# Block-sparse attention and a gated expert layer on one core: turning P by transposing transfers from the second batch on

## The chip, the cores and the metric

The kernel runs on one core of a Trainium2 chip. The metric is the device time of one launch in microseconds (us), the median of several runs. Engines are named as in the profile: PE is the matmul engine (PEld its weight loads), DVE and ACT are the vector and the scalar engine, POOL is GpSimd, SP only issues transfers.

## The reference

Attention over 4 batches, 8 heads, 768 positions, head width 64. Positions lie in 24 blocks of 32. A query block sees its own block and both neighbours, the first and the last block, and three sampled blocks of its own; the first and the last query block see everything. The result is laid out as 3072 tokens of 512 features and goes through a gated layer of width 1536.

```
scores = q @ k.T / sqrt(64); masked where the block pattern says so
attn   = softmax(scores);  x = attn @ v          # -> [3072, 512]
out    = (sigmoid(x @ w_gate) * (x @ w_val)) @ w_out
```

Input and output are float32; the kernel works in float16 with float32 sums.

## The kernel before

**An order that is written out by a planner.** The kernel doesn't write its instructions in the order in which they will run. It declares operations (`P(name, engine, duration, function, deps, prio, acq, rel)`), each with an engine, an assumed duration, a priority and the buffers that it takes and gives back. `Planner.run` (line 69) then plays them through with these durations: at each step it takes the engine that can start first and, of its ready operations, the one of lowest priority number. The order that comes out is fixed in the program for each engine. At run time an engine takes its instructions in just that order, and waits where an input isn't there yet. A transfer is assumed to end `dma` after its issue, plus 1.8 us.

**Attention, by batch.** `attention(b, ...)` (line 430) declares a batch. Batch b has the priority base 10 b, so batches follow each other, with the loads of the next ones ahead (`PREP`). K, Q and V come in through POOL's queue, cast to float16, into three stage buffers `stg`. PE turns K and Q tile by tile (L456), and copies put them into `KT` and `QT` (L466 to L474). `QT` holds zeros in half of its rows, so that one matmul treats two heads. V is reordered by DVE (`vsh`, L486) and written to a scratch tensor in HBM (`scr`, L495, four issues on SP), from which SP reads it back: neighbouring blocks as windows into `V1` (L542), the three sampled blocks one by one into `V2` (L587, with the block number in a register). `V1` and `V2` exist once for even and once for odd batches. `VN` is the whole V of a batch, for the dense rows (L500).

The 22 sparse query blocks of a batch go in 12 steps of one or two blocks (`S0` for batch 0, `S1` for the others; `S1` puts the blocks at the edges first). For each block PE writes the mask with four matmuls from `mrow` (L608) and adds the scores with eight (L614), in an array shape of 128 by 64. A block takes one bank of PSUM; two banks (`spool`) serve for it. DVE finds the row maxima (`mx`, L626), ACT takes the exponential (`ex`, L635), DVE the reciprocal (L643), and POOL or DVE scales P (`sl`, L651, L654). Then P must be turned, so that its columns lie on partitions: PE transposes it against an identity, four 128x128 pieces per block (`tp`, L666), and DVE or ACT copies the piece from PSUM to `PTS` (`te`, L673). PE forms P V (`pv`, L686), and ACT or DVE copies the result to `XT` (`xe`, L701).

The first and the last query block are the dense rows. They are treated for two heads at a time: scores against all of K (L714), maximum, exponential, scale (`dsc` to `dsl`), six transposes into PSUM (`dtp`, L751), a copy to `DPT` (L756), six matmuls with `VN` (`dpv`, L764). In batches 1 to 3 they have the lowest priority numbers of their batch, in batch 0 they come after two thirds of it.

**The expert layer.** The 24 tiles of 128 tokens are cut into `GROUPS`. A group's gate and value matmuls (L814, 12 column blocks of 4 matmuls each) have 128, 256 or 512 columns; tanh on ACT (L822), the product on DVE (L827), then the output matmuls (L840) and a store per tile from one of two buffers `YS` (L847 to L854). The groups have priorities above 1000, so the plan uses them to fill PE where attention leaves it idle, once their tiles are done.

Of the kernel before, what the change touches and what calls it, by code (L numbers as in the profile page):

```python
# [18 lines left out]
BLK = 32  # L19
# [29 lines left out]
class Planner:  # L49
# [19 lines left out]
    def run(self, switch=0.095, dma_lat=1.8):  # L69
# [112 lines left out]
def kernel(  # L182
# [28 lines left out]
    cst = np.zeros((1, NB, 8), np.float32)  # L211
# [3 lines left out]
    cst_h = nc.inline_tensor(cst, name="bb_cst")  # L215

# [8 lines left out]
    def sb(name, shape, dt=f16):  # L225
# [5 lines left out]
    ones = sb("ones", [128, 128], bf16)  # L231
    cst_t = sb("cst", [1, NB, 8], f32)
    sbi = sb("sbi", [1, NB * 3 * 2], i32)
    kidx = sb("kidx", [1, 128], i32)
    vidx = sb("vidx", [1, 128], i32)
# [7 lines left out]
    QT = [sb(f"QT{r}", [128, NP, NB + 1, 64]) for r in range(2)]  # L243
# [4 lines left out]
    VN = sb("VN", [128, 6, DM])  # L248
    V1 = {(r, x): sb(f"V1{r}{x}", [128, n, DM]) for r in range(2) for x, n in (("A", 4), ("B", 3))}
    V2 = {(r, x): sb(f"V2{r}{x}", [128, n, DM]) for r in range(2) for x, n in (("A", 4), ("B", 3))}  # L250
    NKG = 4
    KG = [[sb(f"KG{r}{s}", [128, NP, 160]) for s in range(NKG)] for r in range(2)]
    NPB = 6
    PB = [sb(f"P{s}", [128, 2, 256]) for s in range(NPB)]
# [3 lines left out]
    PTS = [sb(f"PTS{s}", [128, 1024]) for s in range(2)]  # L258
    DP = [sb(f"DP{s}", [128, S]) for s in range(2)]
    DPT = [sb(f"DPT{s}", [128, S]) for s in range(2)]  # L260
# [9 lines left out]
        [(0, 0), (0, 5), (1, 0), (1, 5)],  # L270
        [(1, 1), (1, 2), (1, 3), (1, 4)],
        [(2, 0), (2, 5), (2, 1), (2, 2)],
        [(2, 3), (2, 4), (3, 0), (3, 5)],
        [(3, 1), (3, 2), (3, 3), (3, 4)],
    ]

    XL = sb("XL", [128, 2 * NP, 512])
    XT = [sb(f"XT{g}", [128, NP, 128 * len(G)]) for g, G in enumerate(GROUPS[:-2])]
    XT += [XL[:, 0:NP, :], XL[:, NP : 2 * NP, :]]
    V0 = XL.rearrange("p a n -> p (a n)")[0:TP, 0 : H * TJ * D]  # L280
# [6 lines left out]
    W0 = [(4, 4, "A"), (8, 3, "B"), (11, 4, "A"), (15, 3, "B"), (18, 2, "A"), (1, 3, "B"), (20, 3, "A")]  # L287
    W1 = [(1, 3, "B"), (20, 3, "A"), (4, 3, "B"), (7, 4, "A"), (11, 3, "B"), (14, 4, "A"), (18, 2, "B")]
# [7 lines left out]
    WCH, WOH = 4, 3  # L296
    SCALE_ENG, SCALE_DUR = ("POOL", "DVE"), (0.9, 0.42)
# [5 lines left out]
    def f_const_dma(o):  # L303
        pin(nc.sync.dma_start(sbi, sampled_blocks.bitcast(i32).rearrange("(x a) b -> x (a b)", x=1)))
        pin(nc.sync.dma_start(cst_t, cst_h.ap()))
        pin(nc.sync.dma_start(ident, ident_h.ap()))

    c_dma = P("cdma", "SP", 1.9, f_const_dma, prio=-100, lat=2.2)

    def f_memset(o):  # L310
        pin(nc.gpsimd.memset(ones, 1.0))
        pin(nc.gpsimd.memset(mrow, 0.0))

    def f_mask(o):
# [17 lines left out]
        pin(V.tensor_scalar(mrow[0:1, :, 2:5], in0=m3, scalar1=NEG, scalar2=None, op0=ALU.mult))  # L332
        pin(V.tensor_scalar(mrow[0:1, :, 0:2], in0=cst_t[:, :, 3:5], scalar1=NEG, scalar2=None, op0=ALU.mult))

    o_ms = P("memset", "POOL", 0.5, f_memset, prio=-40)
    o_mask = P("mask", "DVE", 3.1, f_mask, deps=[c_dma, o_ms], prio=-100)

    def f_qz(r):
        def f(o):
            pin((nc.vector if o.eng == "DVE" else nc.gpsimd).memset(QT[r].bitcast(f32), 0.0))  # L340
        return f

    o_qz = [P(f"qz{r}", "DVE" if r == 0 else "POOL", 2.7, f_qz(r), prio=-90 if r == 0 else 3) for r in range(2)]
# [64 lines left out]
    FF = {"w": None, "vn": None}  # L408
# [4 lines left out]
    spool = bk(0, 1)  # L413
# [16 lines left out]
    def attention(b, prio0, ldeps):  # L430
# [5 lines left out]
        if b == 0:  # L436
            ldk, hk = load("k", k, b, pp - 0.050, ldeps, np_)
            ldq, hq = load("q", q, b, pp - 0.049, ldk[-1:], np_)
            ldv, hv = load("v", v, b, pp - 0.048, ldq[-1:])
            FF["w"] = weights(ldv[-1])  # L440
        else:
            ldv, hv = load("v", v, b, pp - 0.050, ldeps)
            ldk, hk = load("k", k, b, pp - 0.049, ldv)
            ldq, hq = load("q", q, b, pp - 0.048, ldk)

        kops, qops = [], []
        for nm, ld, hs, res in (("k", ldk, hk, kops), ("q", ldq, hq, qops)):
            for p in range(NP):
# [13 lines left out]
                def f_ev(o, nm=nm, p=p, h=h):  # L462
# [4 lines left out]
                    else:  # L467
                        for hh in range(2):
                            x = slice(64 * hh, 64 * hh + 64)
                            dst = QT[r][x, p, 1:, 32 * hh : 32 * hh + 32].rearrange("d b (j c) -> d b j c", c=4)  # L470
                            if o.eng == "DVE":
                                pin(nc.vector.tensor_scalar(dst, in0=ps[x], scalar1=0.125, scalar2=None, op0=ALU.mult))
                            else:
# [3 lines left out]
                             deps=[tr] + ([o_qz[r]] if nm == "q" else []), prio=pp - 0.040, rel=[h]))  # L477

        def f_q23(o):
            pin(nc.gpsimd.tensor_copy(QT[r][:, :, 0, :].bitcast(f32), QT[r][:, :, NB, :].bitcast(f32)))  # L480

        q23 = P(f"q23{b}", "POOL", 0.35, f_q23, deps=qops, prio=pp - 0.038)

        def f_vsh(o):
            t = by_head(stg[pl.handles[hv][1]])
            pin(nc.vector.tensor_copy(by_row(V0 if b == 0 else stg[o.slots[f"vsh{b}"][1]]), t.rearrange("p h j d -> p j h d")))  # L486

        vs = P(f"vsh{b}", "DVE", 1.14, f_vsh, deps=ldv, prio=pp - 0.045, rel=[hv],
               acq=[(f"vsh{b}", [("v0", 0)] if b == 0 else stages)])

        def f_scr(o):
            src = V0 if b == 0 else stg[o.slots[f"vsh{b}"][1]]
            dst = scr[b].rearrange("(b j c) n -> c b j n", j=TJ, c=4)
            for c in range(4):
                pin(nc.sync.dma_start(dst[c], src.rearrange("(b c) (j n) -> c b j n", c=4, j=TJ)[c]))  # L495

        sc = P(f"scr{b}", "SP", 2.0, f_scr, deps=[vs], prio=pp - 0.045, dma=2.2, ndma=3, rel=[f"vsh{b}"])

        def f_vn(o):
            pin(nc.sync.dma_start(VN, scr[b].rearrange("(t p) n -> p t n", p=128)))  # L500

        vn = P(f"vn{b}", "SP", 0.5, f_vn, deps=[sc], after=[FF["vn"]], prio=bp - 1.2 + (0.5 if b == 0 else 0), dma=2.3,
               acq=[(f"vn{b}", [("vn", 0)])])
        FF["vn"] = vn

        steps = S0 if b == 0 else S1
        wins = W0 if b == 0 else W1
        step_of = {i: y for y, st in enumerate(steps) for i in st}
        wprio = {}
        for i0, n, x in wins:  # L510
            wprio.setdefault(x, bp + 0.1 * step_of[i0] - 1.5)
        vfl = {}
        def f_fl(o):
            pin(nc.sync.dma_start(V1[r, "A"][96:128, 0, :], scr[b][0:BLK, :]))
            pin(nc.sync.dma_start(V2[r, "A"][0:BLK, 0, :], scr[b][S - BLK : S, :]))

        fl = P(f"vfl{b}", "SP", 1.0, f_fl, deps=[sc] + v_users[b - 2], prio=min(wprio.values()) - 0.05, dma=0.2, ndma=2)
        for x, n in (("A", 4), ("B", 3)):
            def f_fc(o, x=x, n=n):
                n0 = 1 if x == "A" else 0  # L520
                for vt, ps in ((V1, slice(96, 128)), (V2, slice(0, BLK))):
                    pin(nc.gpsimd.tensor_copy(
                        vt[r, x][ps, n0:n, :].bitcast(f32),
                        vt[r, "A"][ps, 0:1, :].bitcast(f32).broadcast_to([BLK, n - n0, DM // 2])))

            vfl[x] = P(f"vfc{b}{x}", "POOL", 2.0, f_fc, deps=[fl], prio=wprio[x] - 0.05)

        def f_kfl(o):
            for s in range(NKG):
# [370 lines left out]
```

## Time and profile before

| | us |
|---|---|
| median of 3 runs | 369.84 (369.13 to 370.27) |
| profiled execution, own time | 371.52 |
| its span, first to last instruction | 369.6 |
| PE busy | 326.2 |
| DVE busy | 256.0 |
| ACT busy | 218.3 |
| POOL busy | 106.8 |
| granted PE clock, mean | 0.957 |

The hardware queue (SP's transfers) moved 30.20 MB, 28.8% of the time of the 16 transfer engines over the span; the software queue (POOL's) 14.16 MB, 24.4%. The costliest rows of attention on PE are the scores (L614, 704 matmuls, 66.3 us busy), the turns of P (L666, 352, 29.3 us) and the mask (L608, 352, 26.1 us). Busy times of PE overlap at their ends, because matmuls are pipelined; the distance between two starts is the better price. Shares over the whole span are averages: the first 40 us load and start, until 140 us the loads of all batches run, from 305 us on only the expert layer is left.

### The profile page before, as it was taken

Reading aid. Unit: us, or ns where it says so; the run is one execution under the profiler, and the core shown is the slowest. Engines: PE = TensorE matmul, PEld = TensorE weight load, DVE = VectorE, ACT = ScalarE, POOL = GpSimd, SP = SyncE. Lnnn points to the kernel's source line nnn. Section 1 sums busy time; section 2 is a strip of 40 time slices with the busy share of each in tenths; the row PEclk is TensorE's granted clock in tenths of the full one; section 3 lists DMA queues with packets and bytes.
Section 4 is the critical chain, followed back from the end, with each engine's and each line's share of the span. In section 5 each row is a group of like instructions: output and inputs, shape, how many; then the busy total and the mean of one; then the engine's idle time right before and its main releaser. Section 6 shows DMA issues by size and latency. Waiting matters only on the chain.

```text
span 369.6 us, 11338 instructions
## 1 busy us (share of the span) xinstructions
PE 326.2 (88%) x3904; PEld 203.1 (55%) x3904; DVE 256.0 (69%) x686; ACT 218.3 (59%) x662; POOL 106.8 (29%) x361
## 2 busy tenths in 40 slices
PE   2745968989789689999799999999999999999995
PEld 2634756757666544566366556555655654444442
DVE  8697747778688869689469999668989833402320
ACT  3566546774687746767477777877775653313321
POOL 8457470116333553212005234002574100000000
PEclk9995789999999869999899999999999999999999
DMA  7947899997979893125343623331133430011002
GB/s 123 205 115 208 156 212 231 218 243 157 228 188 203 165 268 73 45 67 162 101 118 109 168 73 98 115 94 38 46 89 87 139 104 2 1 59 57 0 30 86
DMA packets 47262, 45.09 MB, mean 122 GB/s; under 512 B 5986, under 2 KB 44132, under 8 KB 47204
## 3 DMA queue, kind: packets, MB, share of 16 engines
q1 hardware_dynamic: 31956, 30.20, 28.8%
q0 software_dynamic: 15248, 14.16, 24.4%
q8 instruction: 31, 0.51, 0.6%
q14 instruction: 27, 0.22, 0.2%
HBM read 49.06 MB, written 9.44 MB: 158 GB/s over the span
## 4 chain that ended last, share of the span: by engine, by line
PE 63%; DVE 14%; DMA 11%; issue 4%; ACT 4%; SPq 2%; POOL 0%; POOLq 0%; DVEq 0%; ACTq 0%
PE bank L814 28%; PE bank L840 17%; PE bank L686 4%; DMA stg<-in_q_dram 4%; PE bank L614 4%; DVE NM L626 4%; PE bank L666 4%; PE bank L608 3%; DVE P L654 2%; DMA wv<-in_moe_w_val_dram 2%; DMA V10A<-scr 2%; DVE HT L827 2%; DMA V21A<-scr 2%; DMA scr<-stg 1%; DVE m L326 1%
## 5 line engine op out<-in xcount | busy, mean ns | idle before, releaser
L635 ACT ACTIVATE P<-bank,NM 128x256 f16<-128x256 f32 x176 | 81.5, 473 | 27.2 <-DVE NM L626 22.1
L827 DVE SCALAR_TENSOR_TENSOR HT<-TH,bank 128x512 f16<-128x512 f32 (+2 forms) x96 | 52.6, 551 | 48.2 <-PE bank L814 43.5
L822 ACT ACTIVATE TH<-bank 128x512 f32<-128x512 f32 (+2 forms) x96 | 46.9, 493 | 54.8 <-PE bank L814 46.0
L573 POOL COPY KG<-KT 128x64 f32 x264 | 51.0, 239 | 96.5 <-PE bank L614 89.1
L840 PE MATMUL bank<-wo,HT 128*128 128x512 f16 x288 | 66.8, 386 | 3.3 <-ACT YS L849 2.5
L626 DVE TENSOR_REDUCE NM<-bank 128x2 f32<-128x512 f32 x88 | 59.0, 684 | 3.7 <-PE bank L614 3.2
L814 PE MATMUL bank<-XT,wv 128*128 128x512 f16 (+2 forms) x288 | 55.2, 316 | 2.1 <-DMA wv<-in_moe_w_val_dram 2.0
L814 PE MATMUL bank<-XT,wg 128*128 128x512 f16 (+2 forms) x288 | 55.5, 317 | 0.8 <-DMA wg<-in_moe_w_gate_dram 0.3
L814 PEld LDWEIGHTS <-wv 128*128 128x128 f16 x384 | 32.9, 99 | 27.3 <-DMA wv<-in_moe_w_val_dram 2.1
L840 PEld LDWEIGHTS <-HT 128*128 128x128 f16 x288 | 27.7, 99 | 35.4 <-issue 5.9
L814 PEld LDWEIGHTS <-wg 128*128 128x128 f16 x384 | 32.5, 100 | 25.8 <-issue 1.9
L654 DVE TENSOR_SCALAR P<-P,ZZ 128x256 f16<-128x256 f16 x150 | 38.3, 300 | 2.3
L608 PE MATMUL bank<-mrow,ones 128*64 128x96 bf16 (+2 forms) x352 | 26.1, 227 | 11.4 <-ACT P L635 8.5
L635 ACT ACTIVATION_READ_ACCUMULATOR P<-bank,NM 128x1 f32 x176 | 35.7, 203 | 0.0
L614 PE MATMUL bank<-KG,QT 128*64 128x160 f16 x352 | 34.3, 249 | 0.1
L614 PE MATMUL bank<-KT,QT 128*64 128x96 f16 x352 | 32.0, 218 | 0.4 <-ACT QT L474 0.4
L666 PE MATMUL bank<-ident,P 128*128 128x128 f16 x352 | 29.3, 229 | 2.3 <-ACT QT L474 1.3
L673 DVE COPY PTS<-bank 128x1024 f16<-128x1024 f16 (+1 forms) x37 | 23.6, 643 | 10.6 <-PE bank L666 10.5
L608 PEld LDWEIGHTS <-ones 128*64 128x64 bf16 x352 | 16.5, 115 | 25.7 <-issue 13.3
L849 ACT ACTIVATE YS<-bank 128x512 f32<-128x512 f32 x20 | 11.9, 597 | 29.4 <-PE bank L840 22.7
L614 PEld LDWEIGHTS <-QT 128*64 128x64 f16 x704 | 27.6, 119 | 0.9 <-ACT QT L474 0.7
L666 PEld LDWEIGHTS <-P 128*128 128x128 f16 x352 | 23.6, 103 | 8.1 <-issue 3.0
(91 smaller groups left out, 476.0 us busy)
## 6 DMA issues: line engine op xcount, KB each, us to landing
out_dram<-YS SPq DMA_DIRECT2D x24, 256.0 KB
stg<-in_v_dram POOLq DMA_DIRECT2D x4, 768.0 KB, 10.3
VN<-scr SPq DMA_DIRECT2D x4, 768.0 KB
V20A<-scr SPq DMA_DIRECT2D x74, 32.0 KB
stg<-in_k_dram POOLq DMA_DIRECT2D x3, 768.0 KB, 10.5
stg<-in_q_dram POOLq DMA_DIRECT2D x3, 768.0 KB, 14.8
scr<-stg SPq DMA_DIRECT2D x12, 192.0 KB
V21A<-scr SPq DMA_DIRECT2D x68, 32.0 KB
```

Of the source, the lines that this page charges most:

```text
L573: pin(nc.gpsimd.tensor_copy(t[:, :, (2 + n) * BLK : (3 + n) * BLK].bitcast(f32), KT[r].bitcast(f32)[:, :, bass.ds(vals[(i % 8) * 3 + n], B ...
L608: pin(nc.tensor.matmul(t[64 * hp : 64 * hp + 64, a, 256 - w : 256], ones[:, 0:64], mv, start=(a == 0), stop=False, skip_group_check=True))
L614: pin(nc.tensor.matmul(t[64 * hp : 64 * hp + 64, a, c0:c1], QT[r][:, p, 1 + i, :], src[:, p, :], start=False, stop=True, skip_group_check= ...
L626: pin(nc.vector.tensor_reduce(NM[o.slots[hz][1]][:, 0:2], t, axis=AX.X, op=ALU.max, negate=True))
L635: pin(nc.scalar.activation(pb[:, a, :], t[:, a, :], AF.Exp, bias=NM[z][:, a : a + 1], scale=1.0, accum_out=ZZ[z][:, a : a + 1]))
L654: pin(nc.vector.tensor_scalar(pb[:, a, :], in0=pb[:, a, :], scalar1=ZZ[z][:, a : a + 1], scalar2=None, op0=ALU.mult))
L666: pin(nc.tensor.transpose(t[:, u * 512 + c * 128 : u * 512 + c * 128 + 128], pb[:, c * 128 : c * 128 + 128], ident))
L673: pin(copy(o)(PTS[pl.handles[hTS][1]][:, 0:n], banks[o.slots[hT][1]].bitcast(f16)[:, 0:n]))
L814: pin(nc.tensor.matmul(t, wt[:, c, f_ * 128 : f_ * 128 + 128], XT[g][:, c, :], start=(c == 0), stop=(c == 3)))
L822: pin(nc.scalar.activation(TH[o.slots[ht][1]][:, 0:n], banks[o.slots[hg][1]][:, 0:n], AF.Tanh, bias=0.0, scale=0.5))
L827: pin(nc.vector.scalar_tensor_tensor(HT[:, f_, hoff : hoff + n], in0=TH[o.slots[ht][1]][:, 0:n], scalar=1.0, in1=banks[o.slots[hv][1]][:, ...
L840: pin(nc.tensor.matmul(t, HT[:, f_, hoff + tt * 128 : hoff + tt * 128 + 128], wo[:, f_, :], start=(f_ == 0), stop=(f_ == NF - 1)))
```

## The change

- **P turned by transfers.** In batches 1 to 3 (`TURN_DMA = 1`) the transposes and the copies behind them are replaced by one transposing transfer per step, issued on SP, from P in SBUF to `PTS` in SBUF, up to 128x1024. The dense rows the same, 128x1024 (their columns are padded from 96 to 128 in each of eight pieces). Batch 0 keeps the transposes on PE. `PTS` has four buffers for two, P four buffers of a step for six of a block.
- **Scores of a step in one piece.** One operation writes the mask and the scores of both blocks; the mask takes two matmuls of up to 192 columns per block for four of up to 96. `spool` has three banks.
- **Value buffers shared.** `V1` and `V2` become four buffers in turn for all batches. The rows of the first and the last block are filled in again for each batch and buffer. `VN` goes: the dense rows multiply with the reordered V in its stage buffer (eight matmuls of 96 rows for six of 128), which stays taken until then. The V of batch 0 lies in `QT[1]`, and `QT[1]` is zeroed after the last dense product of batch 0. Gathers of batch 0 may go through POOL.
- **Order.** All batches use the steps `S0`; dense rows come at priority 0.8, 0.3, 0.3, 0.3 of their batch. Batch 0 loads K, V, Q for K, Q, V. The first weights wait for the issue of `scr`.
- **Expert groups.** One group of 512 columns becomes two of 256 (sizes 1, 1, 2, 2, 2, 4, 4, 4, 4 tiles), and `XT` becomes a ring of twelve tiles that is used twice.

The core of the diff:

```diff
-    def run(self, switch=0.095, dma_lat=1.8):
+    def run(self, switch=0.12, dma_lat=1.8):
...
-        [(0, 0), (0, 5), (1, 0), (1, 5)],
-        [(1, 1), (1, 2), (1, 3), (1, 4)],
-        [(2, 0), (2, 5), (2, 1), (2, 2)],
-        [(2, 3), (2, 4), (3, 0), (3, 5)],
-        [(3, 1), (3, 2), (3, 3), (3, 4)],
+        [(0, 0), (0, 5)],
+        [(1, 1), (1, 2)],
+        [(1, 3), (1, 4), (1, 0), (1, 5)],
+        [(2, 1), (2, 2), (2, 3), (2, 4)],
+        [(2, 0), (2, 5), (3, 1), (3, 2)],
+        [(3, 3), (3, 4), (3, 0), (3, 5)],
...
+    V0 = QT[1].rearrange("p a b n -> p (a b n)")[0:TP, 0 : H * TJ * D]
...
+    STEPS = [S0, S0, S0, S0]
...
+    DENSE = [0.8, 0.3, 0.3, 0.3]
...
+    TURN_DMA = 1
+    VGATHER = [(("SP", "POOL"), (1.5, 1.0))] + [("SP", 1.5)] * 3
...
-    spool = bk(0, 1)
+    spool = bk(0, 1, 2)
...
             ldk, hk = load("k", k, b, pp - 0.050, ldeps, np_)
-            ldq, hq = load("q", q, b, pp - 0.049, ldk[-1:], np_)
-            ldv, hv = load("v", v, b, pp - 0.048, ldq[-1:])
-            FF["w"] = weights(ldv[-1])
+            ldv, hv = load("v", v, b, pp - 0.049, ldk[-1:])
+            ldq, hq = load("q", q, b, pp - 0.048, ldv[-1:], np_)
+            FF["w"] = weights(ldq[-1])
...
+                    n0, n1 = (0, 4) if i == 1 else (1, 5) if i == NB - 2 else (1, 4)
+                    mv = mrow[:, i, n0:n1].unsqueeze(1).unsqueeze(3).broadcast_to([128, 2, n1 - n0, BLK])
+                    for hp in range(2):
+                        pin(nc.tensor.matmul(t[64 * hp : 64 * hp + 64, :, 96 + n0 * BLK : 96 + n1 * BLK], ones, mv,
+                                             start=True, stop=False, skip_group_check=True))
...
+            sc_ = P(f"sc{b}_{st[0]}", "PE", 0.27 * len(st) + 0.06, f_sd, deps=[kgs[i][0] for i in st] + kops + qops + [o_mask], prio=pr, mode=64,
+                    acq=[(hS[i], early if b == 0 and si < 2 else spool) for i in st], rel=[kgs[i][1] for i in st])
...
+            pts = [("pts", s) for s in range(NTS)]
+            if b < TURN_DMA:
...
+            else:
+
+                def f_td(o, st=st, hP=hP, hTS=hTS):
+                    n = len(st)
+                    pin(nc.sync.dma_start(PTS[o.slots[hTS][1]][:, 0 : 4 * n, :],
+                                          PB[o.slots[hP][1]].rearrange("p u a n -> p (u a n)")[:, 0 : 512 * n], transpose=True))
+
+                te = P(f"td{b}_{st[0]}", "SP", 0.5, f_td, deps=sls, prio=pr - 0.05, acq=[(hTS, pts)], rel=[hP], dma=0.6 * len(st))
...
-            pr = bp + (0.8 + 0.02 * p if b == 0 else 0.01 * p - 0.05)
+            pr = bp + DENSE[b] + 0.02 * p
...
+                    pin(nc.tensor.matmul(banks[o.slots[h][1]][:, 0:384], QD[r][:, p, :],
+                                         KT[r][:, p, :].rearrange("d (b j c) -> d j b c", j=TJ, c=4)[:, c0 // TP : c0 // TP + 4],
+                                         start=True, stop=True))
...
+                def f_dtd(o, hDP=hDP, hTS=hTS):
+                    pin(nc.sync.dma_start(DPT[o.slots[hTS][1]], DP[o.slots[hDP][1]].rearrange("q j p -> q (j p)"), transpose=True))
+
+                dte = P(f"dtd{b}{p}", "SP", 0.5, f_dtd, deps=[dl], prio=pr - 0.05, acq=[(hTS, dpts)], rel=[hDP], dma=1.0)
...
+                for j in range(TJ):
+                    pin(nc.tensor.matmul(t, vrows(o)[:, j * DM + p * 128 : j * DM + p * 128 + 128], d[:, j * 128 : j * 128 + 128],
+                                         start=(j == 0), stop=(j == TJ - 1)))
...
+        if b == 0:
+            for o in o_qz[1]:
+                o.deps.extend(dpvs[0] + scr_ops)
...
+        for o in {id(o): o for bt in G for o in xops[bt]}.values():
+            for x in REUSE.get(g, ()):
+                o.deps.extend(lastv[x])
```

## The prediction

> **What bounds the kernel now.** I read the page's busy table and slices first. The three numbers to see are PE's 88%, the strip of nines in the PE row from the middle on, and the DMA row, which is full in the first third and below half afterwards.
>
> ```profile
> PE 326.2 (88%) x3904; PEld 203.1 (55%) x3904; DVE 256.0 (69%) x686; ACT 218.3 (59%) x662; POOL 106.8 (29%) x361
> ...
> PE   2745968989789689999799999999999999999995
> ...
> PEclk9995789999999869999899999999999999999999
> DMA  7947899997979893125343623331133430011002
> ```
>
> Then the busy time of each engine in four stretches (columns: length, PE, PEld, DVE, ACT, POOL busy, clock, DMA share, GB/s).
>
> ```profile
> 140.00:305.00 165.00, 160.50 (x1982) 95.52 (x1981) 132.55 (x364) 114.50 (x354) 43.20 (x167) 0.99 0.34 95
> 305.00:369.60 64.60, 59.45 (x289) 26.91 (x287) 15.82 (x23) 18.53 (x32) 0.00 (x0) 0.99 0.09 33
> 0.00:40.00 40.00, 21.81 (x367) 18.36 (x368) 32.51 (x77) 20.91 (x63) 25.34 (x83) 0.84 0.84 166
> 40.00:140.00 100.00, 84.42 (x1272) 62.31 (x1271) 75.12 (x225) 64.38 (x215) 38.27 (x111) 0.93 1.03 207
> ```
>
> From 140 us to the end PE is idle for 4.5 + 5.2 us of 230 at a clock of 0.99, so there a microsecond of PE work is a microsecond of time. Before 140 us the limits are loads (DMA 1.03) and start-up. Last I read the chain of waits in one stretch of steady state, for what one visit of PE costs.
>
> ```profile
> 210.17 0.21 PE bank L608 x4
> 210.38 0.22 PE bank L614 x8
> 210.60 0.97 PE bank L814 x4
> ...
> 213.43 0.45 PE bank L666 x8
> ...
> 215.75 0.86 PE bank L814 x4
> ...
> 223.49 0.09 PE bank L608 x4
> 223.58 0.22 PE bank L614 x8
> ```
>
> Eight turns take 0.45 us, 56 ns each. A block of scores takes 0.43 us, but 0.31 when it follows another block (the last two lines), and the expert matmuls behind scores take 0.97 instead of 0.86. So each separate visit to the scores costs 0.12 + 0.11 = 0.23 us for changing the array's shape.
>
> **The change part by part, on PE.** (1) Turns of P, batches 1 to 3: 3 x 22 blocks x 4 = 264 transposes x 56 ns = 14.8 us go. (2) Turns of the dense rows there: 12 x 6 x 56 ns = 4.0 go; in batch 0 eight replace six, 4 x 2 x 56 ns = 0.4 come; the dense product has eight terms for six, 16 x 2 x 56 ns = 1.8 come. (3) Scores of a step in one piece: after 110 us the trace has 54 visits (44 of one block, 10 of two); three batches of 12 steps need 36, so 18 x 0.23 = 4.1 go. Two mask matmuls of 192 columns for four of 96 stream the same columns: nothing. (4) One group of 512 becomes two of 256: the 256-column matmul follows its like at 109 ns, the 512-column one at 216, so 96 pairs cost 0.2 us. (5) The dense scores read K with a stride. No row shows a strided moving operand; the bounds are nothing and the whole of their row again (32 x 128x384, 8.2 us). A faster read has no reason. I take nothing, since the mask row, whose operand repeats an element 32 times, runs four matmuls in 0.09 us. Sum on PE: -14.8 - 4.0 + 0.4 + 1.8 - 4.1 + 0.2 = -20.5 us.
>
> **Off PE.** The copies behind the turns (L673 34.1 us over DVE and ACT, three quarters of it; L756 10.8, the same) leave 34 us of DVE and ACT time. I count nothing for it: DVE is at 132.6 of 165 us. POOL fills eight value buffers per batch for four (16 more of 0.83 us) and gets the zeroing of DP: 14 us under a POOL that has 122 us idle there. Four VN loads go, one constant load comes on SP.
>
> **What takes the turn's place.** 36 step transfers and 12 dense ones, 48 issues on SP, up to 256 KB each, 11.5 MB. Three prices are unknown, because no row of the trace turns data in a transfer.
>
> Issue on SP. Plain issues have these rows:
>
> ```profile
> 18.59 1.85 SPq L495 DMA_DIRECT2D scr<-XL  x2
> ...
> 205.74 4.89 SPq L587 DMA_DIRECT2D V20B<-scr  x9
> ...
> 234.14 0.37 SPq L854 DMA_DIRECT2D out_dram<-YS  x1
> ```
>
> So 0.37 us for a 256 KB store, 0.44 us per gather in a row of them, 0.8 to 0.9 for a cut-up store. From 140 to 305 us SP issues 174 gathers (76 us), 15 windows, 4 scr, some 12 stores: about 90 us. With PE 20 us shorter, 145 - 90 = 55 us are free, 1.15 us for each of 48. Both row prices (18 to 43 us) fit. A cheaper one gains nothing, since SP isn't the bound. I take 0.4, the row of the same size.
>
> Bytes. The 30.2 MB of the hardware queue take 28.8% of the span, 3.5 us per MB: 11.5 MB are 40 us of the 16 engines. With 0.34 x 165 = 56 us there now, 96 of 145. [...]
>
> Landing. The plan allots 0.5 + 1.2 + 1.8 + 0.05 = 3.55 us from issue to use for a pair. The 256 KB store lands in 2.05 (last stretch of the chain: "177.82 2.05 DMA out_dram<-YS"), a gather in the loaded stretch in 5.96 ("124.21 5.96 DMA V21A<-scr"). PE's order is written out beforehand, so a late landing stops everything queued behind that P V product: the next scores, the expert matmuls. With scores 1.5 steps ahead about every second of 48 visits shows the delay, 24 us per us late. After 140 us I take 2.05 to 3.5: covered. From 110 to 140 us, where batch 1 begins under the last loads, I take 2.4 us late on 8 visits, half shown: between 0 and 19, taken at 4 because the stretch has little else waiting and the expert groups of batch 0 fill it.
>
> [...] This trace has 56 ns per turn on PE and nothing for the DMA.
>
> **Waits that are added.** The transfer stands on SP behind the scale, and behind it stand gathers (issued some 14 steps ahead), output stores (two YS buffers) and the next scr. K and V of batch 0 now come before Q: V's chain (vsh, scr, gathers) starts some 3.8 us earlier, the first scores as much later, since by their landing marks the first loads come in at 1.9 us per 384 KB; these cancel. V0 now lies in QT1, so zeroing QT1 (2 x 1.4 us on POOL) and the Q evictions of batch 1 wait for the last dense product of batch 0; before, that product ran from 72 to 94 us and the Q tiles of batch 1 were turned from 83 to 87, so up to 94 + 2.8 - 87 = 10 us can show. The fourth expert group needs batch 0 alone and fills that gap; I take 0. XT is a ring of twelve tiles: a slot is written again twelve tiles, or 93 us of expert work, later (31.1 us of PE for four tiles at the end of the chain), so I take nothing for it. DENSE later only reorders.
>
> **Sum.** Profiled execution 371.5 us (span 369.6); - 20.5 + 4 = 355.0. It stands 1.7 us above the median of the runs, so the forecast is 353.5, said as 354.
>
> **The rivals.** *SP becomes the bound* (slower). SP carries the gathers, so a dearer issue adds 48 times its excess over 1.15 us. Equal time is at (165 - 90) / 48 = 1.56 us. At twice the dearest row, 1.6 us, it is 354 + 48 x 0.45 = 376, at 1.9 us 390. For: a turn moves elements and the dearest row is the most cut-up transfer. Against: every row is at half that. [...]
>
> *Late landings.* Each us over 3.55 costs 24. Half a us to 1.4 us late gives 366 to 388; equal time at 0.65 us. For: 5.96 us in the loaded stretch. Against: the share after 140 us is 0.34, and gathers there land in 1.8 us.
>
> *Far late.* Turns land like the crowded loads, 10 us and more (v loads: 10.3): 6.8 x 24 = 163 more, about 517. [...] Against: 256 KB at 2.05.
>
> *The front loses.* QT1 waits out the dense rows in full, or Q comes late: 10 us, 364. Still faster.
>
> *More than the sum.* The freed copies shorten the loop scale to P V and the 4.5 us idle go, with 4 us of the front: 345.
>
> **How the numbers follow.** Forecast 0.46 (347 to 360), more than the sum 0.08, the front 0.10; SP 0.15; late landings 0.17 (0.05 faster, 0.03 equal, 0.09 slower); far late 0.04. Faster 0.46 + 0.08 + 0.10 + 0.05 = 0.69; same 0.03; slower 0.15 + 0.09 + 0.04 = 0.28. Same means within 0.3%, 1.1 us, about what a measurement of this kernel tells from nothing. The range 341 to 388 leaves out far late, the upper half of SP and a little below. The forecast's own range is 347 to 360.
>
> **What would show it.** Right: no L666-like rows after batch 0, PE near 305 us busy and still nines to the end, transposing issues under 1.1 us on SP, landing by 3.5 us, and scores in runs of 20 matmuls. Wrong: PE's row below nine after 140 us with PE waiting for the turned P (landing), SP rows end to end (issue), or a DMA row near ten.

## The result, and the profile after

The changed kernel takes 414.3 us (median of four runs, 411.8 to 414.9) against 369.5 for the kernel before, a ratio of 1.121 with a 95% interval of 1.114 to 1.128: 45 us slower. The profiled execution has a span of 413.1 us. From the page, busy times, slices, the packet count, the hardware queue and the shares of the chain:

```profile
PE 319.4 (77%) x3528; PEld 200.5 (49%) x3528; DVE 237.4 (57%) x672; ACT 213.5 (52%) x681; POOL 123.4 (30%) x382
...
PE   2444798887588989937567798959779877999995
...
PEclk9975879999988999979959889969899899999999
DMA  7995999737998699793667545756465645202002
...
DMA packets 91002, 53.76 MB, mean 130 GB/s; under 512 B 53346, under 2 KB 87554, under 8 KB 90946
...
q1 hardware_dynamic: 75218, 37.93, 42.0%
...
PE 38%; DMA 29%; SPq 13%; issue 7%; DVE 4%; ACT 4%; POOL 4%; POOLq 0%; DVEq 0%; ACTq 0%
```

The strip of nines is gone: PE is busy 319.4 us, 6.8 less than before, and idle 93.7 instead of 43.4. Those two differences are the whole of the span's +43.5 us. The change takes work from PE and returns seven times as much in waiting. In the chain SP's share goes from 2 to 13% and that of transfers from 11 to 29%. The three stretches from 40 us on (columns as before: length, PE, PEld, DVE, ACT, POOL busy, clock, DMA share, GB/s) show where:

```profile
40.00:140.00 100.00, 81.42 (x1210) 63.70 (x1209) 73.81 (x217) 63.88 (x209) 50.27 (x136) 0.91 0.91 168
140.00:305.00 165.00, 128.01 (x1391) 77.00 (x1389) 103.40 (x301) 93.52 (x321) 44.40 (x160) 0.90 0.69 135
305.00:369.60 64.60, 55.16 (x503) 28.96 (x504) 32.53 (x84) 29.41 (x95) 5.70 (x30) 0.97 0.41 94
```

From 140 to 305 us PE was idle for 4.5 us before and is idle for 37 now. What it waits for is in the waits of PE (engine, line, releaser: us in total, times, longest), first after, then the gathered rows before:

```profile
PE bank L744 <- DMA V<-scr: 29.5, 23, 5.1
PE bank L498 <- DMA stg<-in_k_dram: 11.8, 3, 7.1
PE bank L834 <- DMA DPT<-DP: 6.9, 5, 2.4
...
PE bank L744 <- DMA PTS<-P: 0.5, 1, 0.5
```

```profile
PE bank L686 <- DMA V20A<-scr: 2.4, 3, 1.1
PE bank L686 <- DMA V21A<-scr: 2.0, 1, 2.0
...
PE bank L686 <- DMA V20B<-scr: 0.4, 2, 0.2
```

The product of P and V (L744) waits 29.5 us for V's rows, 4.8 in the kernel before (L686), and only 0.5 us for the P that the new transfers turn. This is the largest row, and its 25 us more are half of the 50 us by which PE's idle time grew; the rest is spread over smaller rows. The rows point away from the new transfer, at the old one that stands behind it on SP. SP's own rows in one piece of steady state (start, us, instruction, how many):

```profile
208.12 1.25 SPq L730 DMA_TRANSPOSE PTS<-P  x1
209.46 1.30 SPq L826 DMA_TRANSPOSE DPT<-DP  x1
210.85 1.29 SPq L730 DMA_TRANSPOSE PTS<-P  x1
214.51 2.87 SPq L638 DMA_DIRECT2D V<-scr  x6
...
218.32 1.26 SPq L730 DMA_TRANSPOSE PTS<-P  x1
219.78 3.00 SPq L638 DMA_DIRECT2D V<-scr  x6
222.97 2.62 SPq L826 DMA_TRANSPOSE DPT<-DP  x2
225.64 3.77 SPq L540 DMA_DIRECT2D scr<-stg  x4
```

A transposing issue holds SP for 1.2 to 1.3 us here; over the kernel (duration in ns: lowest, median, highest):

```profile
L730 SPq DMA_TRANSPOSE PTS<-P x36: 1202/1256/3246, 104.6 to 350.7; - x36
```

The rows of SP stand almost end to end, and what seems to be a hole (212.1 to 214.5) is one register load of 2.13 us, which this view leaves out. The chain of waits at the same place goes from one of SP's gathers to PE and then from a dense turn to PE:

```profile
222.47 1.62 DMA V<-scr
224.09 0.14 issue
224.23 0.07 PE bank L744
224.30 3.99 DMA DPT<-DP
228.29 0.04 issue
228.34 1.04 PE bank L834 x8
```

**How full SP is.** I add up SP's instructions of every kind, register and address work included, with gaps of under 0.25 us between them, over the attention of batches 1 to 3 (from the last P V product of batch 0 to that of batch 3). Some kernels of the experiments stand in the table too.

| kernel | stretch, us | SP occupied, us | share | time, us (median) |
|---|---|---|---|---|
| before | 206 | 161.8 | 79% | 369.5 |
| all turns on PE (e1) | 207 | 161.2 | 78% | 373.4 |
| after | 264 | 245.4 | 93% | 414.3 |
| e1 and 12 dense transfers (g4) | 214 | 183.4 | 86% | 377.8 |
| e1 and 16 transfers in batch 3 (g2) | 212 | 187.5 | 88% | 376.9 |
| e1 and 36 unread transfers (e4) | 247 | 225.0 | 91% | 398.7 |
| e1 and 144 tiny transfers (f1) | 273 | 252.8 | 93% | 432.0 |
| fixed gathers, turns by transfer (f5) | 219 | 163.5 | 75% | 369.2 |
| fixed gathers, turns on PE (f6) | 215 | 60.2 | 28% | 378.3 |
| f6 and 36 unread transfers (g5) | 224 | 127.4 | 57% | 381.5 |

Stretch and occupancy come from the profiled execution, the time from all runs; the profiled executions of e1, e4 and f5 took 3.9, 6.4 and 5.9 us more than the medians, so their rows are rough.

SP was four fifths full before the change. The 48 transposing issues add 245.4 - 161.2 = 84 us, 1.75 us each: 74 are the issues with the gaps behind them, 6 are register loads that take longer than in e1, 3 are the semaphore instructions in front of the issues. Three kernels stop at 91 to 93%. That is a mean and no ceiling: cut at the last P V product of each batch, SP is 87, 99 and 96% occupied in batches 1 to 3 of the changed kernel, and 82, 96 and 54% in e1. So SP had no time to spare in batch 2 even without the new issues, and most of what it had in batch 3.

The stretch grows by 264 - 207 = 57 us. Of this the expert work at the end returns 16 (50 us are left after the attention, 66 in e1), since PE did it in the holes, and batch 0, which ends 3 us earlier than in e1, the rest: 57 - 16 - 3 = 38 us is the difference between the two profiled executions. The medians lie 41 us apart.

### The profile page after: what moved, and what is told of

Its sections match the earlier page's. It is cut to its first block, busy times and chain, and to the rows that moved or that the text cites. A ratio compares the mean times of both kernels' runs of the same rounds, so it can differ in the third digit from the quotient of the medians.

```text
span 413.1 us, 10598 instructions
## 1 busy us (share of the span) xinstructions
PE 319.4 (77%) x3528; PEld 200.5 (49%) x3528; DVE 237.4 (57%) x672; ACT 213.5 (52%) x681; POOL 123.4 (30%) x382
## 4 chain that ended last, share of the span: by engine, by line
PE 38%; DMA 29%; SPq 13%; issue 7%; DVE 4%; ACT 4%; POOL 4%; POOLq 0%; DVEq 0%; ACTq 0%
PE bank L890 17%; PE bank L921 11%; DMA V<-scr 10%; SPq L638 7%; DMA DPT<-DP 5%; DMA stg<-in_k_dram 4%; PE bank L744 3%; DMA stg<-in_v_dram 2%; DMA stg<-in_q_dram 2%; SPq L730 2%; DMA wv<-in_moe_w_val_dram 2%; PE bank L663 2%; PE bank L834 2%; ACT P L686 1%; SPq L540 1%
## 5 line engine op out<-in xcount | busy, mean ns | idle before, releaser
L686 ACT ACTIVATE P<-bank,NM 128x256 f16<-128x256 f32 x176 | 81.4, 475 | 26.1 <-DVE NM L676 14.5
L890 PE MATMUL bank<-XA,wv 128*128 128x512 f16 (+2 forms) x432 | 85.2, 322 | 2.9 <-ACT TH L898 1.6
L890 PE MATMUL bank<-XA,wg 128*128 128x512 f16 (+2 forms) x432 | 84.5, 321 | 2.5 <-DVE HT L903 1.9
L610 POOL COPY KG<-KT 128x64 f32 x264 | 50.6, 238 | 118.6 <-PE bank L663 110.8
L744 PE MATMUL bank<-PTS,V 128*128 128x64 f16 x704 | 35.7, 198 | 43.7 <-DMA V<-scr 29.5
L744 PEld LDWEIGHTS <-V 128*128 128x128 f16 x704 | 29.3, 101 | 55.5 <-issue 24.9
L890 PEld LDWEIGHTS <-wv 128*128 128x128 f16 x432 | 39.6, 102 | 27.9 <-issue 6.5
L890 PEld LDWEIGHTS <-wg 128*128 128x128 f16 x432 | 38.9, 102 | 28.9 <-issue 7.5
L704 DVE TENSOR_SCALAR P<-P,ZZ 128x256 f16<-128x256 f16 x176 | 48.9, 330 | 2.7
L759 ACT CAST XA<-bank 64x256 f16<-64x256 f32 (+1 forms) x68 | 24.4, 360 | 41.1 <-PE bank L744 38.8
L575 POOL COPY V<-FL 32x1024 f32<-32x1024 f32 (+1 forms) x32 | 29.8, 968 | 39.0 <-PE bank L744 19.6
L498 PE MATMUL bank<-ident,stg 96*64 96x96 f16 x512 | 18.7, 231 | 22.9 <-DMA stg<-in_k_dram 11.8
L686 ACT ACTIVATION_READ_ACCUMULATOR P<-bank,NM 128x1 f32 x176 | 36.4, 207 | 0.0
L663 PE MATMUL bank<-KG,QT 128*64 128x160 f16 x352 | 32.4, 247 | 1.2 <-POOL KG L610 1.2
L663 PEld LDWEIGHTS <-QT 128*64 128x64 f16 x704 | 30.8, 119 | 2.1 <-issue 1.4
L663 PE MATMUL bank<-KT,QT 128*64 128x96 f16 x352 | 31.2, 218 | 0.5 <-ACT QT L516 0.5
```

The costliest lines, as they stand in the source:

```text
L575: pin(nc.gpsimd.tensor_copy(vt[x][96:128, 0:n, :].bitcast(f32), FL[96:128, c : c + 1, :].bitcast(f32).broadcast_to([BLK, n, DM // 2])))
L610: pin(nc.gpsimd.tensor_copy(t[:, :, (1 + n) * BLK : (2 + n) * BLK].bitcast(f32), KT[r].bitcast(f32)[:, :, bass.ds(vals[(i % 8) * 3 + n], B ...
L663: pin(nc.tensor.matmul(t[64 * hp : 64 * hp + 64, a, c0:c1], QT[r][:, p, i, :], src[:, p, :], start=False, stop=True, skip_group_check=True))
L686: pin(nc.scalar.activation(pb[:, a, :], t[:, a, :], AF.Exp, bias=NM[z][:, a : a + 1], scale=1.0, accum_out=ZZ[z][:, a : a + 1]))
L704: pin(nc.vector.tensor_scalar(pb[:, a, :], in0=pb[:, a, :], scalar1=ZZ[z][:, a : a + 1], scalar2=None, op0=ALU.mult))
L744: pin(nc.tensor.matmul(t[:, u, p, :], vt[:, ws, p * 128 : p * 128 + 128], pt[:, off : off + 64], start=(c == 0), stop=(c == 1), skip_group ...
```

## The experiments

Three theories: A, SP's time is short, and what is queued behind the new issues comes late; B, the transfers themselves are slow, by landing or by bytes; C, another part of the change costs the time.

### Which part: the turns

**e1, all turns on PE.** The rest of the change stays.

```diff
-    TURN_DMA = 1
+    TURN_DMA = 4
```

> The changed kernel with all turns back on PE (TURN_DMA = 4), everything else of the change kept. Theory A, SP is the bound (48 issues of 1.25 us in front of the gathers): the loss goes, and what is left of the gain is the scores in one piece, 4 us: 362 to 372. Theory B, the turned P lands too late for a fixed order: the same, 362 to 375. Theory C, the loss is in the rest of the change (shared value buffers, order, groups): stays above 395.

373.4 us, 1.012 of before (1.004 to 1.020). 41 of the 45 us are the turning transfers; C falls as the main cause. What is left is some 4 us slower than before, where the sum had given these parts a small gain.

**g4, transfers for the dense rows alone** (12 of the 48), and **g2, transfers in the last batch alone** (16 of 48).

```diff
-            if b < TURN_DMA:      # g4
+            if True:
-    TURN_DMA = 1                  # g2
+    TURN_DMA = 3
```

> The changed kernel with only the dense rows turned by transfers (12 of the 48); the steps of all batches are turned on PE. Theory A: 4 issues of 1.4 us per batch fit into SP's idle time: as with all turns on PE, 368 to 376. Theory B (PE waits for each late landing): a quarter of the loss, 380 to 388.

> The changed kernel with transposing transfers in batch 3 alone (TURN_DMA = 3): 16 of the 48. Theory A: each batch has SP work of its own, about 54 us in 68; with 22 us more, batch 3 alone is over and pays a third of the 41 us: 382 to 392. If only the sum over all batches counted, 162 + 22 us in 207 would fit: 370 to 376. Theory B: a third too, so this run tells the two readings of A apart and not A from B.

377.8 us (1.023, 1.016 to 1.031) and 376.9 (1.020, 1.012 to 1.029): 4.5 and 3.5 us over e1, hardly more than the runs of e1 scatter (371.5 to 377.2), where their shares of 41 would be 10 and 14. They add 22 and 27 us to SP (table). The cost isn't proportional to the count: where SP has time to spare, the issues cost little here. g2's sixteen stand in batch 3, which e1 leaves at 54%; there SP is at 90% now.

### SP's time or the transfers

**e4, turns on PE, and the 36 step transfers as well, into a buffer that nobody reads.**

```diff
-    TURN_DMA = 1
+    TURN_DMA = 4
...
+                    P(f"td{b}_{st[0]}", "SP", 0.5, f_td, deps=sls + [tp], prio=pr - 0.05,
+                      acq=[(f"J{b}_{st[0]}", [("jk", s) for s in range(2)])], rel=[hP, f"J{b}_{st[0]}"], dma=0.6 * len(st))
```

> The turns on PE as in the run with TURN_DMA = 4, and beside them the 36 step transfers of batches 1 to 3 are issued as well, on SP, into a buffer that nobody reads (no dense ones). Theory A (SP is the bound): SP is as loaded as in the changed kernel, so the time is near it, 395 to 415. Theory B (PE waits for the turned P): nobody waits for it here, 362 to 378. Theory C: above 395 whatever is turned where.

398.7 us (1.079, 1.071 to 1.088), 25 us over e1. No engine waits for the result, so PE's waiting for a landing can't be this cost. Still open: SP's time or bytes.

**f1, turns on PE, and four tiny transfers per step on SP** (16 x 16 bytes each).

```diff
+                        for x in range(k, k + 4):
+                            pin(nc.sync.dma_start(JK[0:16, x * 8 : x * 8 + 8], ident[0:16, 0:8]))
```

> The turns on PE, and for each step of batches 1 to 3 four tiny transfers (16 rows of 16 bytes, into a buffer that nobody reads) are issued on SP where the transposing one would stand: SP is held some 1.5 us per step, and next to no data moves. Theory A (the time of SP is what is short): as slow as the run with shadow transfers, 390 to 402. Theory B (what the turned data does in the transfer engines is what costs): as the run with the turns on PE, 372 to 378.

432.0 us (1.169, 1.158 to 1.179), 59 us over e1, with next to no bytes. The tiny issues at their line (min/median/max in ns), and the largest wait of PE:

```profile
L730 SPq DMA_DIRECT2D JK<-ident x144: 507/587/1554, 104.8 to 359.3; - x144
```

```profile
PE bank L751 <- DMA V<-scr: 46.8, 28, 6.2
```

This shows A by itself: the same wait as in the changed kernel, and a larger loss. It is above the range that was expected because the tiny issues add 92 us to SP (table), some 2.5 us per step and not 1.5. The loss follows the time that is added to SP's 161 us in e1: 22 and 27 us cost 4.5 and 3.5 (g4, g2), 64 cost 25 (e4), 84 cost 41 (after), 92 cost 59 (f1).

**g5, the converse: room on SP, turns on PE, and the 36 unread transfers**; its partner without them is **f6**, and **f5** is the changed kernel with the same room. Room is made by a fixed gather: one transfer of 96 rows at a fixed place per block, without register loads on SP. These kernels leave out the sampling, so they answer a question and can't be kept.

```diff
-                    vals = regs[(b, "SP", i // 8)]
-                    for n in range(3):
-                        pin(nc.sync.dma_start(V2[x][n * BLK : (1 + n) * BLK, ws, :],
-                                              scr[b][bass.ds(vals[(i % 8) * 3 + n], BLK), :]))
+                    pin(nc.sync.dma_start(V2[x][0:96, ws, :], scr[b][i * 24 : i * 24 + 96, :]))
```

> The changed kernel with the three gathers of a block, which take their rows from registers, replaced by one transfer of 96 rows at a fixed place (so the sampled values are not the right ones; the bytes are the same), and without SP's register loads. SP loses two of three gather issues, all address arithmetic and the register loads, some 100 us in all; the transposing transfers stay on SP. Theory A: the forecast comes back, 345 to 365. Theory B: 395 to 412.

> The same fixed gathers with the turns on PE: the control. Theory A: SP is not quite the bound with the turns on PE, so it gives 365 to 373, and the run with fixed gathers and transposing transfers lies 10 to 20 below it. Theory B: 365 to 373, and the other lies above it.

> Fixed gathers (one transfer per block at a fixed place, so the sampled values are not the right ones) and no register loads on SP, turns on PE, and the 36 step transfers issued beside them into a buffer that nobody reads: the traffic of the turns without a shortage on SP. Theory A: as the run with fixed gathers and turns on PE, 375 to 382. Theory B (the transposed traffic itself slows loads, gathers or engines): 395 or more, since the same traffic on the busy SP gave 25 us.

f6 takes 378.3 us (1.023), g5 381.5 (1.032, 1.024 to 1.039): with room, the 36 unread transfers cost 3 us, not 25. That is all that their bytes and packets cost there. f5 takes 369.2 us (0.996, 0.992 to 1.001): with room, turning by transfer is 9 us better than turning on PE, landings included. B falls. Its PE waits:

```profile
PE bank L498 <- DMA stg<-in_q_dram: 13.5, 3, 4.9
PE bank L498 <- DMA stg<-in_k_dram: 12.7, 3, 7.2
PE bank L741 <- DMA PTS<-P: 8.2, 7, 2.2
```

PE's work falls by 17.5 us against f6 (323.4 to 305.8), and 8.2 us are spent waiting for turned P. The difference of the two is near the 9 us, but other waits differ too and the two profiled executions lie only 4.9 us apart.

**e2, the gathers of all batches on POOL**, another way to make room.

```diff
-    VGATHER = [(("SP", "POOL"), (1.5, 1.0))] + [("SP", 1.5)] * 3
+    VGATHER = [(("SP", "POOL"), (1.5, 1.0))] + [("POOL", 1.0)] * 3
```

> The changed kernel with the value gathers of all batches given to POOL as one indirect transfer per block, so SP loses 198 issues of 0.44 us (87 us) and keeps the transposing ones. Theory A (SP is the bound): most of the loss goes, 355 to 375. Theory B (late landings of the turned P): little moves, 400 to 415. Theory C (shared buffers): 400 to 415.

410.1 us (1.112, 1.101 to 1.122). This is where B and C had put it, but it doesn't decide between them and A, since a second queue was loaded: SP falls to 74% and PE's wait for V from 29.5 to 7.6 us, but an indirect gather takes POOL 0.93 us at the median, and K's copies and V's fills stand behind it. In the waits of PE and of POOL:

```profile
PE bank L663 <- POOL KG L610: 13.8, 4, 10.4
```

```profile
POOL V L575 <- DMA V<-scr,rows: 24.1, 5, 16.0
```

**f3, the transposing transfers issued by ACT** instead of SP.

```diff
-                    pin(nc.sync.dma_start(PTS[o.slots[hTS][1]][:, 0 : 4 * n, :],
+                    pin(nc.scalar.dma_start(PTS[o.slots[hTS][1]][:, 0 : 4 * n, :],
...
-                te = P(f"td{b}_{st[0]}", "SP", 0.5, f_td, deps=sls, prio=pr - 0.05, acq=[(hTS, pts)], rel=[hP], dma=0.6 * len(st))
+                te = P(f"td{b}_{st[0]}", "ACT", 1.3, f_td, deps=sls, prio=pr - 0.05, acq=[(hTS, pts)], rel=[hP], dma=0.6 * len(st))
```

> The changed kernel with its 48 transposing transfers issued by ACT instead of SP (the planner is told 1.3 us each). The same data, the same readers. Theory A (SP's time): SP is as free as before, ACT gets 60 us in 260: 352 to 372. Theory B (transfer engines or landing): 395 to 412, as in the changed kernel.

410.0 us (1.107, 1.095 to 1.120), where B had put it. SP is now only 59% occupied, but it waits, in its own rows of the waits, for the very transfers that were moved away:

```profile
SPq L638 <- DMA PTS<-P: 41.6, 11, 10.3
SPq L638 <- DMA DPT<-DP: 23.2, 6, 7.1
```

The gathers at L638 don't read that data. The trace of the changed kernel shows what an issue waits on: SP's 362 transfers count on eight semaphores, and nearly every issue (337 of 362) first waits on the very semaphore that it will count on, so for the transfer that used it last. In f3 the two rows are 17 waits, 64.8 us, that the landing of a transposing transfer of ACT ended; that these count on the same semaphores is my reading of the rows. In the changed kernel, where SP issues all of them, this is one wait of 0.5 us ("SPq L638 <- DMA DPT<-DP: 0.5, 1, 0.5"). So f3 doesn't speak for B: SP was blocked by a wait in place of an issue.

### The plan's costs

The order of all queues is planned from costs that the kernel's source gives. **e3** plans a transposing issue at 1.3 us; **h2** does so in f5 and gives V's cut-up store 3.4 us; **h4** gives the kernel before 3.4 us for that store and 2.0 for its register loads.

```diff
-                te = P(f"td{b}_{st[0]}", "SP", 0.5, f_td, deps=sls, prio=pr - 0.05, acq=[(hTS, pts)], rel=[hP], dma=0.6 * len(st))
+                te = P(f"td{b}_{st[0]}", "SP", 1.3, f_td, deps=sls, prio=pr - 0.05, acq=[(hTS, pts)], rel=[hP], dma=0.6 * len(st))
...
-        sc = P(f"scr{b}", "SP", 2.0, f_scr, deps=[vs], prio=pp - 0.045, dma=2.2, ndma=3)
+        sc = P(f"scr{b}", "SP", 3.4, f_scr, deps=[vs], prio=pp - 0.045, dma=2.2, ndma=3)
```

> The changed kernel with the planner told 1.3 us for a transposing issue instead of 0.5; the instructions are the same and only the order written out can differ. Theory A (SP is the bound): the same issues remain, 400 to 415. Theory B (a fixed order that counts on turned P 0.8 us too early): the P V products are placed later and other work before them, 370 to 395. Theory C: no change, 410 to 418.

> Fixed gathers (the sampled values are not the right ones) and transposing transfers, as in the run that gave 369, with the planner told SP's true costs (1.3 us for a transposing issue, 3.4 for the scr stores). If only the shortage on SP and the fixed order's wrong costs stood between the change and the forecast: 350 to 362. If the 82% of PE that is left there comes from something else (loads of K and Q that PE meets too early, stage buffers held longer): 365 to 375.

> The kernel before, with nothing but the planner's costs for SP made true (3.4 us for the four scr stores, 2.0 for a register load). If the order written out suffers from its costs for SP there too, 360 to 367; if SP at four fifths hides it, 367 to 373.

e3 takes 406.2 us, 8 less than the changed kernel: part of the loss was an order made for cheap issues. The 245 us of SP's work don't fit into 207 in any order. h2 takes 358.1 us (0.970, 0.961 to 0.979), 11 less than f5. Its busy times:

```profile
PE 302.0 (85%) x3528; PEld 193.5 (54%) x3528; DVE 240.7 (68%) x672; ACT 209.3 (59%) x675; POOL 123.4 (35%) x382
```

With room on SP and a plan that knows the price, PE's work falls as forecast and the time by 11 us of the 16. How much of the 11 is the turns isn't shown: neither the kernel before nor f6 was run with both this room and this plan. h4 takes 375.8 us (1.014, 1.006 to 1.022): dearer costs made the kernel before 7 us slower (its register loads take 1.4 us at the median and 1.7 in the mean, so 2.0 is too much there). So an order alone is worth 2 to 3% either way, and a few us between two of these kernels shouldn't be put down to the edit itself.

### The rest of the change

**h1: e1 with each block's scores as a step of its own**, and **h3: e1 with loads in the order K, Q, V.**

```diff
-            sc_ = P(f"sc{b}_{st[0]}", "PE", 0.27 * len(st) + 0.06, f_sd, ...
+            for i in st:                                             # h1
+                sc_of[i] = P(f"sc{b}_{i}", "PE", 0.33, ...
...
-            ldv, hv = load("v", v, b, pp - 0.049, ldk[-1:])           # h3
-            ldq, hq = load("q", q, b, pp - 0.048, ldv[-1:], np_)
+            ldq, hq = load("q", q, b, pp - 0.049, ldk[-1:], np_)
+            ldv, hv = load("v", v, b, pp - 0.048, ldq[-1:])
```

> The run with the turns on PE, with the scores of a step declared block by block again (the mask stays at two matmuls). If a separate visit to the scores costs the 0.23 us that the prediction took, and the 18 visits saved are worth 4 us, this is 3 to 5 us slower than the 373 of that run: 376 to 378. If taking two banks at once costs as much as the visits save, it is the same or faster: 368 to 374.

> The run with the turns on PE, with batch 0 loading K, Q, V again. The prediction let the earlier V and the later Q cancel. If the 4 us by which the first scores come later are paid in full: 368 to 371. If they cancel: 372 to 375. If the earlier V was worth more: above 376.

386.0 us (1.040) and 382.6 (1.031): the scores in one piece are worth some 12 us and the earlier V 9, within e1's order, and a part of either may be the order itself. Of the 12 us, 5.4 are PE's work (327.4 us in h1, 322.0 in e1, at the same clock of 0.964); the others are waits. Yet e1 as a whole is 4 us slower than before. If the two gains add, which no run shows, some 25 us are lost elsewhere in the rest (shared value buffers, V's stage held until the dense product, dense rows late, finer groups). None of these was taken out alone; this stays open.

### In search of a version that beats both

**g1** gives SP's work its measured costs in the plan and lets it divide the gathers between SP and POOL in every batch; **r1** and **r2** turn by transfer in batches 2 and 3 alone and divide the gathers there, with the measured costs and with the old ones for the store and the registers.

```diff
-    VGATHER = [(("SP", "POOL"), (1.5, 1.0))] + [("SP", 1.5)] * 3
+    VGATHER = [(("SP", "POOL"), (1.6, 1.0))] * 4                                                   # g1
+    TURN_DMA = 2                                                                                   # r1, r2
+    VGATHER = [(("SP", "POOL"), (1.5, 1.0)), ("SP", 1.5)] + [(("SP", "POOL"), (1.6, 1.0))] * 2
```

> The changed kernel with the planner told what SP's work takes (1.3 us for a transposing issue, 3.4 for the four scr stores, 2.0 for a register load) and free to give the gathers of any batch to SP or to POOL, whichever it thinks free first. Theory A (SP's time is short; with all gathers on POOL, POOL's queue took its place): the split relieves both, 350 to 372. Theory B (landing and traffic of the turned data): 395 to 412.

> A version meant to be kept: transposing transfers in batches 2 and 3 alone, where the loads are over, their gathers split between SP and POOL by the plan, batch 1 turned on PE with its gathers on SP; the planner has the true costs of SP. Theory A (SP has room in both halves): the run with all turns on PE less 5 us of PE work per batch, 358 to 368. If the split's own loss in batch 1 (its scores took 95 us there instead of 66) is not from batch 1's loads: 375 to 388.

> The same with the planner's old costs for the scr stores (2.0) and the register loads (1.2), since the true ones made the kernel before slower. Theory A: 358 to 370, the difference from its sister being what the order alone does. Otherwise 375 to 388.

387.6 us (1.045), 389.0 (1.054) and 382.6 (1.037). g1 takes 27 us off the changed kernel, 8 of which the price of a transposing issue alone gave (e3); the others are another sign that SP was short. But part of the loss then moves to POOL: in r2 PE waits 8.4 us for one late copy of K behind the gathers ("PE bank L663 <- POOL KG L610: 8.4, 2, 7.9"). No kernel that gathers the sampled rows beat the kernel before.

## Why the prediction was wrong

**The step that failed is "Issue on SP".** Two of its numbers were off, and the second weighs more.

- The price. I took 0.4 us from the row of the same size. The changed kernel's 36 step issues take 1.20 to 3.25 us, 1.26 at the median, and the 48 add 1.75 each to SP with all that hangs on them. The size of the transfer was the wrong likeness.
- The free time. I counted SP's DMA issues alone, about 90 of 165 us, with 0.44 us for a gather where the row that I show has nine in 4.89 us, 0.54 each with their address arithmetic. In the kernel before, between 100 and 306 us and with the small gaps behind them, the gathers' issues are 82 us, but register loads are 25 (14 of 1.8 us), address arithmetic about 27, stores 14 and the rest 14. SP was 79% occupied, not 55%. Two of the rows that the count left out:

```profile
L394 SPq TENSOR_LOAD <-vidx x20: 1414/1436/3502, 4.4 to 294.0; - x20
...
L587 SPq FUSED_REGOPS  x264: 37/37/51, 27.1 to 301.9; - x132
```

At 79%, 130 of the forecast's 165 us were taken, so its equal time was (165 - 130) / 48 = 0.73 us per issue, less than half of the 1.56 it states, and "SP isn't the bound" didn't follow.

The rival "SP becomes the bound" names what happened, and what to look for in SP's rows. By its own arithmetic the measured issue would have given 354 + 48 x (1.26 - 1.15) = 359 us; it stopped at 390 because it inherited the free time from the same count. The size of the transfer made little difference to its issue: six of the 36 steps have one block for two, and yet no issue is shorter than 1.20 us; the last one, at 350.7 us, is of such a step and takes 1.20, where the median of all is 1.26.

**PE's sum was right.** -20.5 us were forecast; h2 has 302.0 us of PE work against 326.2, -24.2, at the same clock. (The step from 355.0 to the median's scale gives 353.3, not 353.5.) In the changed kernel itself only 6.8 show, though it runs the same 3528 matmuls as h2: at a granted clock of 0.916 for 0.957 they took 319.4 us.

**Scores in one piece** were put at 4.1 us, 0.23 us for each of 18 separate visits; in e1's order they are worth some 12, of which 5.4 are PE's work, near the forecast. **K, V, Q: "these cancel"** was wrong too, by 9 us. Both sizes were missed in the change's favour, and something in the same part of the change took them back.

**Bytes** didn't bind, as forecast, but they were dearer. The hardware queue went from 30.2 to 37.9 MB and from 28.8 to 42.0% of the span, that is from 106 to 174 us of the 16 engines, 67 more where the forecast has 40; packets under 512 B went from 5986 to 53346. The 36 step transfers cost 3 us by that (g5 and f6).

**Landing** was near. After 140 us a step's transfer lands 3.73 us after its issue at the median, a dense one 3.81, where the plan allots 3.55; gathers land in 1.66 and a 256 KB store in 2.08 in the same stretch. PE waits 0.5 us for turned P and 6.9 for turned dense rows, so *late landings* is some 7 us of 45 by PE's waits, and *far late* didn't occur. From issue to landing 3.73 against 2.08 us for a store of the same size is 1.65 us slower, half of it the longer issue (1.26 against 0.37 us).

**The front** cost nothing, as taken: batch 0 ends at 99.2 us, 100.1 before. The idle slices begin behind it. **A sign came true**: SP rows end to end was listed as the mark of the wrong case. The mark "PE waiting for the turned P" would have misled; PE waits for what the turns displaced.

## What to carry to other kernels

Before giving a queue new work, add up everything that its engine does there, register loads, address arithmetic and blocking waits as well as issues, and compare the new work with the slack that is left; a queue four fifths full took 22 to 27 us more in 207 at a cost of some 4 us, and 64 us more at a cost of 25. The wait that showed here belonged to the old work queued behind (29.5 us for V's rows), not to the new (0.5 us for turned P). Where an order is written out from assumed costs, a new operation needs a measured one (worth 8 us in e3, 11 in h2 together with the store's). That doesn't hold for every cost: dearer ones for the store and the register loads made the kernel before 7 us slower and r1 6 us slower than r2. Orders alone move a time by 2 to 3%.

## What the runs showed of the hardware that I had not expected

- A transposing issue costs its engine 1.26 us at the median on SP and 1.25 on ACT (f3), for four squares hardly less than for eight (1.20 for the step of one block at 350.7 us); a plain issue of 256 KB costs 0.37, and one of 256 bytes 0.59 at the median (f1).
- A register load of V's indices holds SP for at least 1.4 us and 2.1 at the median in the changed kernel (1.4 in the kernel before), 20 times:

```profile
L429 SPq TENSOR_LOAD <-vidx x20: 1417/2098/2562, 8.8 to 353.6; - x20
```

- An issue on one engine can wait for a transfer that another issued: in f3, 17 waits of SP's gathers, 64.8 us, ended with the landing of a transposing transfer of ACT that they don't read. In the changed kernel SP's 362 transfers count on eight semaphores.
- In two pairs of runs the granted clock was lower where PE waits more, and the same matmuls took longer: 319.4 us at a clock of 0.916 and 302.0 at 0.957 (after and h2, PE idle for 93.7 and 53.3 us); 338.8 at 0.923 and 322.0 at 0.964 (f1 and e1, 92.4 and 52.9). What lowers the clock isn't shown.
